# The first loads of an attention + SwiGLU kernel: which row and which weight slice lead which DMA queue, and one transposition placed a K tile sooner

## The chip, the cores and the metric

The kernel runs on one core of a Trainium2 chip. The metric is the device time in microseconds (us) of one execution; less is better. The engines are named as in the profile: PE (TensorE matmuls), PEld (its weight loads), DVE (VectorE), ACT (ScalarE), POOL (GpSimd) and SP (SyncE, which issues DMAs here). ACT can issue DMAs too, on a queue of its own.

## The reference

A layer norm feeds two branches, and both are added to the input. Shapes: S = 2048 tokens, D = 576, F = 4608, 32 heads of 18, a window of 8 keys with a dilation of 2; all tensors are bf16.

```python
xn = layernorm(x)                                   # over D, no scale or bias
q, k, v = split_heads(xn @ wqkv)                    # wqkv: 576 x 1728
# token s looks at tokens s, s-2, ..., s-14 (masked below 0)
o = softmax(q . k[window] * 18**-0.5) @ v[window]   # per head
out = x + o @ wo + (silu(xn @ w_gate) * (xn @ w_up)) @ w_down
```

## The kernel before

**Tiling.** The 2048 tokens are 16 "rows" of 128 tokens (token p * 16 + r is partition p of row r). Four rows make a chunk `c`. Three phases follow one another on PE: the QKV projection of all 16 rows (`qkv_ps`, L301), then, for each of four chunks, gate and up (`g_ps`, L601) and the down projection together with the attention's output projection (`d_ps`, L630). The attention itself runs on DVE beside the FFN matmuls.

**The QKV phase.** The contraction over D = 576 has four K tiles of 128 and a remainder of 64. `wqkv` is loaded by K tile: `load_w(eng, kt)` (L147) brings slice `kt`, 128 x 1728, 432 KB; for `kt` = 4 it brings the remainder in two DMAs of 108 KB to the two halves of the partitions. `load_x(eng, j)` (L144) brings x row `j`, 128 x 576, 144 KB. The argument `eng` is the engine whose queue issues the DMA; each queue keeps its order. In the profile the x rows are the tile `wd` and the weight slices the tile `hT`, because they lie in memory that the FFN uses later. Before the change the order was:

```python
load_x(nc.scalar, 0)
load_x(nc.sync, 1)
load_w(nc.scalar, 1)
load_w(nc.sync, 0)
make_identity(nc, ident[:])
load_w(nc.sync, 2)
load_x(nc.sync, 2)
load_w(nc.sync, 3)
load_w(nc.sync, 4)
load_x(nc.sync, 3)
```

After these come the x rows 4 to 15 in three DMAs of 576 KB on SP (L165), and later the first gate and up weights (`load_gu(0)`, L182 to L185).

**The start on the engines.** The order of work is written out by hand (`manual_schedule`), from L477 on. PE first runs eleven warm-up matmuls on constants (`warm_pe(10, 1)`). Row 0 is a special case: DVE computes its statistics (L214, L218) and subtracts the mean in two parts (L251, first 128 columns, then the rest), POOL fills the padding (L256), PE transposes K tile 0 and then the others (L262), ACT copies the results to `xcT` (L268; `PP` in the profile), and the QKV matmuls of row 0 go through slices 0, 1, 2 (`p_whole`, whole K tiles of 128 rows). Row 0 is scaled by its standard deviation only when its results leave PSUM (`p_evac`, L365 and L367). Row 1 is normalised and transposed between these matmuls; its first K tile is multiplied before slice 3 and the remainder of row 0.

From row 1 on, `p_row` (L321) issues matmuls of half a K tile (64 partitions) in pairs, on the two halves of the array. It goes twice over two pairs of output groups: `swap` 0 and 1, and `i` 0 and 1 within each, with K tiles 0, 4, 1, 2, 3 in the first and 0, 1, 2, 3 in the second pass. K tile 0 is skipped in both passes where `t` is given, which is the case for row 1 alone. The argument `at = (i, kt)` says after which pair of the second pass the function `between` is called; `turn(r)` is such a function and transposes row `r` (`transp_halves`, L274): ten small PE matmuls (L283) into two PSUM banks, then one copy on ACT and one on DVE (L287) to `xnT`. So row 2 is transposed within row 1, row 3 within row 2, row 4 within row 3. Rows from 5 on are transposed by DMA.

PSUM is a ring of eight banks (pool `ps`): a new tile waits until the tile eight places before it has been read.

Of the kernel before, what the change touches and what calls it, by code (L numbers as in the profile page):

```python
# [70 lines left out]
def kernel(  # L71
# [11 lines left out]
    nc = tc.nc  # L83
# [60 lines left out]
    def load_x(eng, j):  # L144
        eng.dma_start(xc_b[0][:, j:j + 1, :], x_v[:, j:j + 1, :])

    def load_w(eng, kt):  # L147
        if kt < 4:
            eng.dma_start(wqkv[:, kt, :], A_wqkv[kt * P:(kt + 1) * P, :])
        else:  # L150
            for i in range(2):
                eng.dma_start(wqkvr[64 * i:64 * i + 64, :], A_wqkv[4 * P:D, 2 * G * i:2 * G * (i + 1)])

    load_x(nc.scalar, 0)
    load_x(nc.sync, 1)
    load_w(nc.scalar, 1)
    load_w(nc.sync, 0)
    make_identity(nc, ident[:])
    load_w(nc.sync, 2)
    load_x(nc.sync, 2)  # L160
# [35 lines left out]
    def new_ps(name):  # L196
        return ps.tile([P, 512], f32, name=name, tag="ps")
# [18 lines left out]
    def ln_aggr(r):  # L216
        c, j = divmod(r, 4)
        nc.vector.bn_aggr(ln[c][2][:, j, :], sums[r][:].rearrange("p c s -> p (c s)"))  # L218
# [55 lines left out]
    def transp_halves(r):  # L274


        c, j = divmod(r, 4)
        xn = ln[c][1]
        pt = [new_ps("pt") for half in range(2)]
        for kt in range(KT):  # L280
            for half in range(2):
                rows = slice(64 * half, 64 * half + 64)
                nc.tensor.matmul(pt[half][:, kt * 64:(kt + 1) * 64], xn[rows, j, kt * P:(kt + 1) * P],  # L283
                                 ident[rows, rows], start=True, stop=True)
        for half, eng in enumerate((nc.scalar.copy, nc.vector.tensor_copy)):
            lo = r * P + 64 * half
            eng(xnT[:, :, lo:lo + 64], pt[half][:, 0:KT * 64].rearrange("p (k t) -> p k t", t=64))  # L287
# [11 lines left out]
    def p_mm(t, g, kt, half, r, start, stop):  # L299
        rows = slice(0, P) if half is None else slice(64 * half, 64 * half + 64)  # L300
        return nc.tensor.matmul(t[g][:, 0:G], xT_of(r)[rows, kt, :], w_at(g, kt, rows),  # L301
                                start=start, stop=stop)
# [10 lines left out]
    def fence_after(mm):  # L313
        f = nc.gpsimd.engine_nop()
        tc.add_manual_dep(f.ins, mm.ins.name, SYNC, reason="first half done")
        return f

    def fence_before(mm, f):
        tc.add_manual_dep(mm.ins, f.ins.name, SYNC, reason="banks change row tiles")

    def p_row(r, between=None, at=(0, 1), t=None):  # L321


        done = t is not None
        t = t or [None] * NG
        fence = {}
        for swap in range(2):
            for i in range(2):
                for kt in (0, 1, 2, 3) if swap else (0, 4, 1, 2, 3):
                    if done and kt == 0:  # L330
                        continue
                    for half in range(2):
                        g = i + 2 * (half ^ swap)
                        if t[g] is None:
                            t[g] = new_ps("qkv_ps")
                        mm = p_mm(t, g, kt, half, r, swap == 0 and kt == 0, swap == 1 and kt == 3)
                        if swap == 0 and kt == 3 and half == 1:
                            fence[i] = fence_after(mm)
                        if swap and kt == (1 if done else 0) and half == 0:
                            fence_before(mm, fence[i])  # L340
                    if swap and (i, kt) == at and between is not None:
                        between()
        return t
# [130 lines left out]
    def turn(r):  # L474
        return lambda: transp_halves(r)
# [32 lines left out]
    u = [None] * NG  # L508
# [11 lines left out]
    load_gu(0)  # L520
    transp_dma(0)

    p_row(1, turn(2), (0, 2), u)
    ln_aggr(3)
    p_evac(1, u, (0, 1, 2), dve=(1, 2))
    ln_sqrt(3)
# [188 lines left out]
```

## Time and profile before

| | us |
|---|---|
| median of 3 runs (503.34 to 504.67) | 503.36 |
| the profiled execution's own time | 503.82 |
| its span, first to last instruction | 502.0 |
| busy time of PE / DVE / ACT / POOL in it | 498.1 / 329.0 / 200.5 / 2.6 |
| first QKV matmul starts, on the span's scale | 6.06 |
| last QKV matmul ends, gate and up begin | 60.19 |

The span is what the profile's time scale covers; 1.8 us of the execution's time lie around it. "SPq" and "ACTq" are the instruction queues of SP and ACT, where DMAs are issued; q1 and q10 are the DMA queues of SP and ACT. A row of the timeline gives start and length in us, engine, line, operation, output and input with shapes, a count, and, in brackets, for how long the engine was idle before it and what ended that. A run of equal instructions is merged to one row.

### The profile page before, as it was taken

What the parts mean: (1) busy time and instruction counts of PE and PEld (TensorE: products, weight loads), DVE (VectorE), ACT (ScalarE), POOL (GpSimd) and SP (SyncE); (2) the same over time, 40 slices, a digit from 0 to 9 for tenths busy, and PEclk for the clock granted to TensorE, in tenths of its full rate; (3) what the DMA queues carried; (4) which work ended last, traced back from release to release, by engine and by line L of the source; (5) the groups of instructions that cost most, each with busy time, mean ns of one, the idle gap of its engine ahead of it and who ended that gap; (6) DMA issues with size and microseconds to landing.
All of it is one profiled execution on the core that took longest, in us unless ns stands there. A gap on an engine that the chain in (4) does not pass through costs nothing.

```text
span 502.0 us, 13267 instructions
## 1 busy us (share of the span) xinstructions
PE 498.1 (99%) x5795; PEld 330.5 (66%) x5795; DVE 329.0 (66%) x478; ACT 200.5 (40%) x415; POOL 2.6 (1%) x9
## 2 busy tenths in 40 slices
PE   9999999999999999999999999999999999999997
PEld 4666655555799755555899655555999555557996
DVE  5888598898999698999898139995980222221001
ACT  4756657644400255554300445557000454553000
POOL 2000000000000000000000000000000000000000
PEclk9999999999999999999999999999999999999999
DMA  8889988789921045536621154465600335453100
GB/s 313 219 206 228 307 280 280 220 273 309 233 82 61 25 136 193 191 106 225 161 69 43 29 185 146 139 189 157 136 25 14 100 114 178 155 177 38 29 14 25
DMA packets 77186, 75.42 MB, mean 150 GB/s; under 512 B 22708, under 2 KB 72528, under 8 KB 77128
## 3 DMA queue, kind: packets, MB, share of 16 engines
q1 hardware_dynamic: 76840, 73.98, 49.7%
q8 instruction: 45, 0.74, 0.6%
q10 hardware_dynamic: 288, 0.59, 0.4%
q14 instruction: 13, 0.11, 0.1%
HBM read 58.76 MB, written 5.90 MB: 129 GB/s over the span
## 4 chain that ended last, share of the span: by engine, by line
PE 99%; DVE 0%; issue 0%
PE g_ps L601 56%; PE d_ps L630 32%; PE qkv_ps L301 11%; PE warm_ps L174 1%; PE pt L262 0%; DVE ot L644 0%; PE pt L283 0%; PE warm_ps L262 0%; PE warm_ps L177 0%
## 5 line engine op out<-in xcount | busy, mean ns | idle before, releaser
L601 PE MATMUL g_ps<-xnT,gu 64*128 64x512 bf16 x2592 | 280.4, 376 | 0.0
L601 PEld LDWEIGHTS <-gu 64*128 64x128 bf16 x2592 | 147.7, 94 | 131.3
L612 ACT ACTIVATE sg<-g_ps 128x512 bf16<-128x512 f32 x144 | 87.3, 606 | 156.6 <-PE g_ps L601 156.6
L630 PE MATMUL d_ps<-wd,hT 64*128 64x288 bf16 x2304 | 146.9, 283 | 0.0
L630 PEld LDWEIGHTS <-hT 64*128 64x128 bf16 x2304 | 131.3, 94 | 10.5
L614 DVE TENSOR_TENSOR hT<-sg,uc 128x512 bf16<-128x512 bf16 x144 | 60.0, 418 | 93.8 <-ACT uc L613 93.6
L613 ACT CAST uc<-g_ps 128x512 bf16<-128x512 f32 x144 | 85.2, 592 | 0.0
L414 DVE TENSOR_REDUCE PP<-PP 128x64 f32<-128x1152 bf16 x64 | 84.9, 1345 | 0.4
L301 PE MATMUL qkv_ps<-hT,xnT 64*128 64x432 bf16 (+1 forms) x536 | 50.2, 343 | 0.0
L409 DVE TENSOR_TENSOR PP<-QO,Kr 128x2304 bf16<-128x2304 bf16 (+1 forms) x35 | 43.5, 1249 | 7.2 <-DMA Kr<-hT 6.9
L642 DVE TENSOR_TENSOR ot<-d_ps,xr 128x288 bf16<-128x288 f32 x30 | 12.3, 451 | 51.1 <-PE d_ps L630 51.1
L441 DVE TENSOR_TENSOR PP<-Vr,A 128x2304 bf16<-128x2304 bf16 (+1 forms) x35 | 43.2, 1250 | 0.4
L301 PEld LDWEIGHTS <-xnT 64*128 64x128 bf16 (+1 forms) x536 | 30.1, 94 | 18.5 <-ACT xnT L287 0.4
L446 DVE TENSOR_TENSOR PP<-PP 128x2304 bf16<-128x2304 bf16 x24 | 32.5, 1353 | 0.3
L612 ACT ACT_TABLE_LOAD x5 | 6.4, 1283 | 47.3 <-PE g_ps L601 47.2
L630 PE MATMUL d_ps<-wo,xnT 64*128 64x288 bf16 x288 | 23.4, 283 | 0.0
L363 ACT CAST hT<-qkv_ps 128x288 bf16<-128x288 f32 (+2 forms) x58 | 21.2, 428 | 0.5 <-DMA kv_d<-hT 0.5
L630 PEld LDWEIGHTS <-xnT 64*128 64x128 bf16 x288 | 16.4, 94 | 1.2
L434 ACT ACTIVATE PP<-PP 128x1024 f32<-128x1024 f32 x4 | 4.2, 1057 | 31.2 <-DVE PP L430 31.2
L644 ACT CAST ot<-d_ps 128x288 bf16<-128x288 f32 x1 | 0.4, 399 | 38.8 <-PE d_ps L630 38.8
L363 ACT CAST QO<-qkv_ps 128x432 bf16<-128x432 f32 (+1 forms) x30 | 12.3, 410 | 7.4 <-PE qkv_ps L301 7.4
L214 DVE BATCH_NORM_STATS2 stats<-wd 128x6 f32<-128x288 bf16 x32 | 12.9, 444 | 2.9 <-DMA wd<-in_A_x_dram 2.6
(53 smaller groups left out, 91.3 us busy)
## 6 DMA issues: line engine op xcount, KB each, us to landing
gu<-in_B_w_gate_dram SPq DMA_DIRECT2D x36, 512.0 KB, 3.8
gu<-in_B_w_up_dram SPq DMA_DIRECT2D x36, 512.0 KB, 5.1
wd<-in_B_w_down_dram SPq DMA_DIRECT2D x9, 576.0 KB, 6.0
kv_d<-hT SPq DMA_DIRECT2D x5, 576.0 KB, 6.4
gu<-in_B_w_gate_dram SPq DMA_DIRECT2D x36, 64.0 KB, 4.7
gu<-in_B_w_up_dram SPq DMA_DIRECT2D x36, 64.0 KB, 4.4
xr<-in_A_x_dram SPq DMA_DIRECT2D x8, 288.0 KB, 5.1
out_dram<-ot SPq DMA_DIRECT2D x16, 144.0 KB, 1.8
```

The source lines that it names most:

```text
L214: nc.vector.bn_stats(sums[r][:, k, :], xc[:, j, k * HALF:(k + 1) * HALF])
L301: return nc.tensor.matmul(t[g][:, 0:G], xT_of(r)[rows, kt, :], w_at(g, kt, rows), start=start, stop=stop)
L363: (nc.vector.tensor_copy if n in dve else nc.scalar.copy)(*parts[n])
L409: nc.vector.tensor_tensor(prod[:, a:b], QO[:, RT * tt + a:RT * tt + b, :], Kr[:, s:s + b - a, :], op=ALU.mult)
L414: nc.vector.tensor_reduce(L[:, w, rs], prod[:, rs].rearrange("p r (h d) -> p r h d", d=DH), axis=AX.X, op=ALU.add)
L441: nc.vector.tensor_tensor(dst[:, a:b], Vr[:, s:s + b - a, :].rearrange("p r (d h) -> p r d h", h=H), A[:, w, a:b].unsqueeze(2).to_broadcas ...
L446: nc.vector.tensor_tensor(dst, acc, pv, op=ALU.add)
L601: mm = nc.tensor.matmul(ring_ps[j][b][:], gu[rows, slot, k, fc], xnT[rows, kt, tok], start=(swap == 0 and kt == 0), stop=(swap == 1 and kt ...
L612: nc.scalar.activation(sg[:], t[0][:], ACT.Silu)
L613: nc.scalar.copy(uc[:], t[1][:])
L614: nc.vector.tensor_tensor(hT[:, ch * FC + j, :], sg[:], uc[:], op=ALU.mult)
L630: mm = nc.tensor.matmul(t[sub][h][:, 0:HALF], a[rows], w[rows, h * HALF:(h + 1) * HALF], start=(swap == 0 and n == 0), stop=(swap == 1 and ...
```

## The change

Four loads at the head of the two queues change place. x row 0 is issued by SP instead of ACT, ahead of row 1. Slice 0 is issued by ACT, as its first and only load, instead of by SP after row 1. Slice 1 goes from ACT to SP, after row 1. All other loads keep their order on SP. And `turn(2)` is called after K tile 1 of the second pass of row 1, not after K tile 2.

```diff
-    load_x(nc.scalar, 0)
+    load_x(nc.sync, 0)
+    load_w(nc.scalar, 0)
     load_x(nc.sync, 1)
-    load_w(nc.scalar, 1)
-    load_w(nc.sync, 0)
+    load_w(nc.sync, 1)
     make_identity(nc, ident[:])
     load_w(nc.sync, 2)
     load_x(nc.sync, 2)
@@
-    p_row(1, turn(2), (0, 2), u)
+    p_row(1, turn(2), (0, 1), u)
     ln_aggr(3)
```

## The prediction

> **What bounds the kernel now.** I read the page first, then the chain of waits in order of time, then the timeline of the first 20 us, because the diff touches nothing later.
>
> The page's first and fourth parts:
>
> ```profile
> span 502.0 us, 13267 instructions
> PE 498.1 (99%) x5795; PEld 330.5 (66%) x5795; DVE 329.0 (66%) x478; ACT 200.5 (40%) x415; POOL 2.6 (1%) x9
> ...
> PE 99%; DVE 0%; issue 0%
> ```
>
> PE is the chain. The chain in order of time shows where it could still lose anything:
>
> ```profile
> 0.76 4.42 PE warm_ps L174 x10
> 5.18 0.11 PE warm_ps L177
> 5.29 0.21 PE pt L262
> ...
> 6.13 2.25 PE qkv_ps L301 x10
> ...
> 19.67 40.52 PE qkv_ps L301 x444
> 60.19 69.93 PE g_ps L601 x648
> ```
>
> From 19.67 on there is no gap: 444 half-row matmuls in 40.52 us is 0.0913 each, 0.1825 a pair. So the time is (start of the first QKV matmul) + (fixed PE work) + (small stalls before 20 us). Only the first and last term can change, and nothing in this diff shortens the fixed work. The timeline of the start, all engines:
>
> ```profile
> 3.81 0.82 DVE L214 BATCH_NORM_STATS2 stats<-wd 128x6 f32<-128x288 bf16 x2 [2.63 <-DMA wd<-in_A_x_dram]
> ...
> 5.21 0.10 PEld L262 LDWEIGHTS <-wd 128*128 128x128 bf16 x1 [0.51 <-DVE wd L251]
> ...
> 5.54 0.27 ACT L268 COPY PP<-pt 128x128 bf16<-128x128 bf16 x1 [0.34 <-PE pt L262]
> ...
> 5.85 0.31 PEld L301 LDWEIGHTS <-PP 128*128 128x128 bf16 x2
> 6.06 2.31 PE L301 MATMUL qkv_ps<-hT,PP 128*128 128x432 bf16 x10
> ...
> 6.37 0.15 PEld L301 LDWEIGHTS <-PP 128*128 128x128 bf16 x1 [0.21 <-issue]
> ...
> 6.73 1.21 PEld L301 LDWEIGHTS <-PP 128*128 128x128 bf16 x7 [0.21 <-issue]
> ```
>
> A serial line runs from the landing of x row 0 to the first QKV matmul: statistics at 3.81, centring, transposition 5.21, copy 5.54 to 5.81, weight load 5.85, matmul 6.06. DVE sat idle 2.63 us for that landing. Two smaller losses are visible. The load at 5.85 was ready, yet its matmul began at 6.06: in the trace's semaphore records the last share of slice 0 (`wqkv[:, 0]`) landed at 6.02. And the first three matmuls start 0.31, 0.36 and 0.20 apart, where 0.182 is the later pace: the array was still slow until about 6.73 (the warm-up matmuls of 512 columns, 0.43 apart, are at that slow pace throughout). The weight-load timeline shows the place of the second edit:
>
> ```profile
> 12.83 0.49 PEld L301 LDWEIGHTS <-xnT 64*128 64x128 bf16 x8
> 13.70 1.97 PEld L301 LDWEIGHTS <-xnT 64*128 64x128 bf16 x24 [0.37 <-ACT xnT L287]
> ...
> 16.03 3.06 PEld L301 LDWEIGHTS <-xnT 64*128 64x128 bf16 x36
> ```
>
> Row 2's first load waits for the two copies of its own transposition; rows 3 and 4, turned after (0,1), go straight on (36 loads from 16.03 with no idle).
>
> **x row 0 goes to SP, slice 0 leads on ACT's queue.** Before, two 144 KB rows led the two queues:
>
> ```profile
> wd<-in_A_x_dram ACTq DMA_DIRECT2D x1, 144.0 KB, 3.1
> wd<-in_A_x_dram SPq DMA_DIRECT2D x1, 144.0 KB, 3.2
> ```
>
> (issue 0.72 each, landings 3.78 and 3.96). The packet records show one packet per row of a tile, eight to an engine, a 1152-byte one every 0.047 us and a 3456-byte one every 0.132, and the two queues taking turns packet by packet: on one engine q10, q1, q10, q1 at 2.526, 2.573, 2.620, 2.667, and with long packets q1, q10, q1 at 3.256, 3.388, 3.520. So x row 0 shared with x row 1 for 16 x 0.047 = 0.75 us; now it shares with slice 0: 8 x (0.047 + 0.132) = 1.43. That is 0.68 later. SP's row landed 0.18 behind ACT's of the same issue time; I add half, 0.09. Sum +0.77. High end 0.68 + 0.18 = 0.86. Low end: SP served entirely ahead of ACT, so that row 0 skips the 8 x 0.047 of the other row: -0.38. I take 0.77, since the taking of turns is in the records. Landing then about 4.55.
>
> [...]
>
> Slice 0, issued at 0.72 and not 1.18 and no longer behind a row, finishes with row 0, near 4.6. Its wait (5.85 to 6.06) goes: -0.20, ends 0 and -0.21. The DVE, ACT and PE line between simply shifts with row 0. First QKV matmul: 6.06 + 0.77 - 0.20 = 6.63.
>
> **What else moves in the queues.** SP now issues x0, x1, w1, w2 ...: from w2 on everything is one issue later (0.40 to 0.46 a row). The transfers run back to back from 2.6 us, so the backlog covers this: w3 was issued at 2.63 and landed at 9.09. The bytes ahead of each slice are the old ones in another order. Slice 1 becomes the fourth item in, as slice 0 was: about 6.1, used by the fifth matmul (7.12 before, about 7.5 now). Row 1 lands 8 x 0.047 after row 0, about 4.95; DVE wants it at 5.39 + 0.77. Slack of the rest, landing against first use: slice 2 7.16/7.85, row 2 7.59/8.72, slice 3 9.09/9.69, the remainder 9.83/10.52, row 3 10.19/11.98, the next x block 11.62/14.90. Slice 3 is thinnest, 0.60, and its user itself comes later; were that cover gone, each microsecond would be one on PE. SP's later issues wait for landings of the first ones (that at 3.80 for row 0's semaphore), so the last pieces are issued about 1 us later, still 3 us ahead of their packets' turn; `gu`, behind them, is wanted at 60. ACT loses one issue, and its table load (1.64, 1.28 us) moves 0.4 ahead; its first use is at 4.90. All this I cost at nothing.
>
> **Clock.** The slow pace ended at about 6.73 in the profiled execution. With the first matmul at 6.63, the three slow starts (0.87 us for 0.55 of work) shrink to one tenth: -0.27, if the pace rises at the same moment. Ends 0 (an execution in which it had risen before 6.06 loses nothing now) and -0.33.
>
> **Row 2 a K tile sooner.** The ten transpositions go in one pair earlier: 0.18. Row 1's last matmul before the boundary starts 0.32 before row 2's first, not 0.18, so 0.13 is lost. Between transposition and boundary lay four pairs of matmuls (`p_row` skips K tile 0 of a row that is begun): 4 x 0.18 + 0.13 = 0.86 was needed, and five pairs give 0.91. All 0.13 comes back, just. Covers: row 2's input was ready at 10.98, transposed from 12.54; ACT's and DVE's earlier work ends at 12.60 and 12.79, and the copies can start near 12.85. The two PSUM banks are row 0's first two, last read by the first of ACT's pair at 11.69 (until 12.19): against 12.36 that cover is thin, 0.17, and if it goes the transpositions wait and the 0.13 stays lost. Ends 0 and -0.14.
>
> **Sum.** Against the profiled execution (503.82, span 502.0): +0.77 - 0.20 - 0.27 - 0.13 = +0.17, 504.0. The median of the runs, 503.36, lies 0.46 lower, which fits executions whose array was fast before 6.06; for those the clock term is nil and the sum is +0.44. With half of the clock term: 503.36 + 0.44 - 0.14 = 503.66, say **503.7**. 0.3% is 1.5 us, about what a measurement of this kernel can tell from no change: this is no change.
>
> **Rivals.**
>
> *The clock stays slow (slower).* Warm-up ends at 5.08 by its own pace, and the first transposition began at 5.21. Now PE would sit idle from 5.08 to about 5.95. If whatever raises the pace wants PE kept busy, those 0.87 us, where 0.13 stood, can cost it. Price from rows: before, it took from 0.76 to 6.73, 6.0 us of nearly steady work. If the earning starts afresh after the gap, the pace rises at up to 11.9 and half of 6.63 to 11.9 is lost, 2.6; if half is kept, about 1.3 to 1.6. So 505.0 to 506.3, about 505.3. It decides from the point where the idle stretch spoils the count; the trace shows only that 0.13 + 0.20 + 0.14 of gaps did not. One of the three runs is 1.3 above the others, which may be this very thing happening now and then.
>
> [...]
>
> *Row 0 isn't held up.* If SP's small packets win, the term of 0.77 falls to between 0 and -0.38, and the gain is 0.2 + 0.13 and up to 0.38: 502.7 to 503.2, still within 0.3%. Against it: the alternating packets.
>
> *A real gain over 1.5 us* has no source: all losses before 20 us add up to less than 1.
>
> **Numbers.** Forecast as summed 0.51; row 0 not held up 0.11; clock stays slow 0.35; something unforeseen ahead 0.03. The first two are "same", 0.62; slower 0.35; faster 0.03. The forecast's own range is 503.1 to 504.4 (ends of the terms). To leave out no more than 2 in 10 the range takes in most of the clock case: 503.0 to 505.7.
>
> **What would show it.** Right: DVE's first statistics near 4.6; first QKV matmul near 6.6, with no gap between its load and itself; weight loads from then on 0.18 apart; no idle ahead of row 2's loads; `g_ps` starting about 0.2 later than 60.19. Wrong: statistics at 3.8 (no sharing); QKV matmuls 0.36 apart until 9 or 12 (clock); an idle PEld before the matmuls of slice 1 or 3 (late slices).

## The result and the profile after

The changed kernel took 505.94 us (median of 6 runs, 505.21 to 506.62), the kernel before in the same comparison 503.62 (503.32 to 504.67). The ratio is 1.0045, 95% interval 1.0033 to 1.0057: slower by 2.3 us, and outside the range of 503.0 to 505.7. A second comparison, below, gave 504.72 (12 runs, 504.14 to 506.91) against 503.81, ratio 1.0027 (1.0014 to 1.0040). So it is slower both times; how much, we shall see, is drawn anew in each execution.

The profiled execution took 506.01, span 504.2. Its chain in order of time, to be read against that of before:

```profile
0.72 4.27 DMA wd<-in_A_x_dram
...
5.01 0.83 DVE stats L214 x2
...
6.73 0.40 PE pt L262 x4
7.13 3.21 PE qkv_ps L301 x10
...
11.33 3.65 PE qkv_ps L301 x30
...
21.80 40.52 PE qkv_ps L301 x444
62.32 69.93 PE g_ps L601 x648
```

Before, the last row stood at 60.19: the whole difference, 2.13, is there when gate and up begin. Three pieces account for it. The first ten QKV matmuls begin at 7.13 instead of 6.13: +1.00. From there to the row at 11.33 (9.02 before) it is 4.20 instead of 2.89: +1.31. From there to 21.80 (19.67 before) it is 10.47 instead of 10.65: -0.18. The first is x row 0, 1.20 later, less slice 0's wait of 0.20, which is gone; the chain now starts with a DMA. The second is the clock, and the third the earlier turn of row 2.

The timeline of weight loads shows the second piece:

```profile
6.42 0.10 PEld L262 LDWEIGHTS <-wd 128*128 128x128 bf16 x1 [1.98 <-DVE wd L251]
6.73 0.23 PEld L262 LDWEIGHTS <-wd 128*128 128x128 bf16 x4 [0.21 <-DVE wd L251]
7.01 0.75 PEld L301 LDWEIGHTS <-PP 128*128 128x128 bf16 x5
7.97 0.15 PEld L301 LDWEIGHTS <-PP 128*128 128x128 bf16 x1 [0.21 <-issue]
8.33 0.15 PEld L301 LDWEIGHTS <-PP 128*128 128x128 bf16 x1 [0.21 <-issue]
8.69 0.15 PEld L301 LDWEIGHTS <-PP 128*128 128x128 bf16 x1 [0.21 <-issue]
```

Five loads go at the fast pace, then each is 0.36 after the last, with nothing to wait for ("issue"). The view by stretches says why (stretch, its length, PE's busy time and matmuls, the granted clock as a share of full speed, the busy share of the DMA engines, GB/s):

```profile
6.00:7.00 1.00, 0.50 (x5) 1.00 0.99 380
7.00:8.00 1.00, 1.00 (x8) 0.76 1.06 400
8.00:9.00 1.00, 1.00 (x4) 0.50 1.03 313
9.00:10.00 1.00, 1.00 (x4) 0.50 1.12 266
10.00:11.00 1.00, 1.00 (x6) 0.53 1.04 399
11.00:12.00 1.00, 1.00 (x9) 1.00 1.01 406
```

The clock, fast from 4.10, was halved from 7.52 to 10.93 by the trace's clock record. Between 4.78, when the warm-up ended, and 6.42 PE had been idle (the chain's owner was DMA). So in this execution the fast clock wasn't late, as the clock rival had it: it came and was taken away again. Each run's mean granted clock shows how often. A halved stretch of 3.41 us in 504 makes it 0.997, and two of the six runs (506.01, 506.62) have that. The other four have 1.0, which doesn't exclude a late first release: in the profile before, the clock record begins with the release at 6.76, and the mean is 1.000 although the first three QKV matmuls start 0.31 and 0.36 apart.

### The profile page after: what moved, and what is told of

Read it like the earlier page. It is cut to its first block, busy times and chain, and to the rows that moved or that the text cites. A ratio compares the mean times of both kernels' runs of the same rounds, so it can differ in the third digit from the quotient of the medians.

```text
span 504.2 us, 13267 instructions
## 1 busy us (share of the span) xinstructions
PE 498.6 (99%) x5795; PEld 285.3 (57%) x5795; DVE 329.1 (65%) x478; ACT 200.6 (40%) x415; POOL 2.6 (1%) x9
## 4 chain that ended last, share of the span: by engine, by line
PE 98%; DMA 1%; DVE 0%; issue 0%
PE g_ps L601 55%; PE d_ps L630 32%; PE qkv_ps L301 11%; DMA wd<-in_A_x_dram 1%; DVE stats L214 0%; PE pt L262 0%; DVE wd L251 0%; DVE ot L644 0%; PE pt L283 0%; DVE mv L218 0%; PE warm_ps L262 0%
## 5 line engine op out<-in xcount | busy, mean ns | idle before, releaser
L601 PEld LDWEIGHTS <-gu 64*128 64x128 bf16 x2592 | 127.0, 94 | 152.1
L630 PEld LDWEIGHTS <-hT 64*128 64x128 bf16 x2304 | 113.1, 94 | 28.7
L301 PEld LDWEIGHTS <-xnT 64*128 64x128 bf16 (+1 forms) x536 | 26.1, 94 | 22.3 <-ACT xnT L287 0.2
L630 PEld LDWEIGHTS <-xnT 64*128 64x128 bf16 x288 | 14.1, 94 | 3.6 <-DMA xnT<-QO 0.2
```

What stands on the lines that cost most here:

```text
L601: mm = nc.tensor.matmul(ring_ps[j][b][:], gu[rows, slot, k, fc], xnT[rows, kt, tok], start=(swap == 0 and kt == 0), stop=(swap == 1 and kt ...
L630: mm = nc.tensor.matmul(t[sub][h][:, 0:HALF], a[rows], w[rows, h * HALF:(h + 1) * HALF], start=(swap == 0 and n == 0), stop=(swap == 1 and ...
```

## The experiments

Each was timed beside the kernel before, in 7 to 12 runs. E10, E11, E8 and E9 share one comparison, E1 to E4 another, E5 to E7 a third; E12 has its own. Theory A: row 0 lands about 1 us later because it takes turns with long packets, and the idle PE then costs the fast clock in many executions. The rivals B to F are in the expectations.

**E1, the loads alone.**

```diff
-    p_row(1, turn(2), (0, 1), u)
+    p_row(1, turn(2), (0, 2), u)      # on the changed kernel
```

> The change with its load order alone; row 2 is turned after (0, 2) as before. Theory A (two terms: row 0 lands about 1 us later because it takes turns with slice 0's long packets, and the idle PE then loses the fast clock for a stretch): the whole loss of 2.3 us is in the loads, so this stands 2.3 to 2.6 us above the kernel before, with a stall of about 0.13 ahead of row 2's loads again. Rival B (the earlier turn of row 2 does harm, by banks or by a late copy): this comes back towards the kernel before, under +1.5 us.

504.74 (504.09 to 505.79), ratio 1.0016 (1.0007 to 1.0025). Only +1.0: under theory A's window, and as rival B had it, 1.2 under the changed kernel. In the profiled run (505.79) the clock was first released at 9.71, against 6.76 in the kernel before: here the clock was late, in the form that the rival had. Side by side, though, the two kernels are alike:

**E10 and E11, the changed kernel and its loads alone, once more and together.**

> The changed kernel itself once more, beside its loads alone and beside a variant without the gap. Theory A (row 0 later by about 1 us; the idle PE then costs the fast clock in many but not all executions): between 504.1 (clock kept) and 506.6, median 504.7 to 506.0, and the same as its loads alone within 0.4. Rival B (the early turn of row 2 does harm together with the late loads): over 1 us slower than its loads alone, as the first two comparisons, made apart, had it (505.9 against 504.7).

> The loads alone, row 2 turned after (0, 2), beside the changed kernel. Theory A: 0 to 0.3 us above the changed kernel on the same chip (the stall of 0.13 is back), 504.7 to 506.0. Rival B: over 1 us below it.

504.72 and 504.82 (504.28 to 506.02; ratio 1.0020, 1.0010 to 1.0029). Rival B is out. The runs of the changed kernel fall into two groups: seven lie between 504.14 and 504.75, five between 505.63 and 506.91, and none between. (With the loads alone the groups are less sharp: E1 and E11 have single runs at 505.00, 505.07 and 505.24.) Two of the upper five have a mean clock of 0.997; the others, with 1.0, were not profiled. The profiled run, of 504.14, kept its clock:

```profile
6.24 0.10 PEld L262 LDWEIGHTS <-wd 128*128 128x128 bf16 x1 [1.69 <-DVE wd L251]
6.55 0.23 PEld L262 LDWEIGHTS <-wd 128*128 128x128 bf16 x4 [0.21 <-DVE wd L251]
6.83 1.57 PEld L301 LDWEIGHTS <-PP 128*128 128x128 bf16 x10
```

All ten loads go at the fast pace. Its `g_ps` starts at 60.50 against 62.32, so one kernel differs from itself by 1.82 us: 0.18 is row 0 (statistics at 4.84, not 5.01), and 1.67 lies between the start of the QKV matmuls and the second mark (2.53 here, 4.20 there). Its idle stretch on PE is a little shorter. The matmuls, first in the changed kernel's first profile, then here:

```profile
6.42 0.70 PE L262 MATMUL pt<-ident,wd 128*128 128x128 bf16 x5 [1.65 <-DVE wd L251]
6.25 0.71 PE L262 MATMUL pt<-ident,wd 128*128 128x128 bf16 x5 [1.36 <-DVE wd L251]
```

And PE's busy time (third figure) in the 3.41 us after each release of the clock:

```profile
4.10:7.52 3.42, 1.70 (x12) 1.00 1.03 375
4.33:7.74 3.41, 1.97 (x13) 1.00 1.01 385
```

With 1.70 busy the clock was lost at the end of the stretch, with 1.97 it was kept. All six runs of the first comparison lie above 505.2. By E10's share, five in twelve, six out of six would come up about once in 200 times, so the share probably differs between comparisons; what sets it was not tested. Setting that high median against E1's, taken apart from it, misled.

**E2, the turn alone.**

```diff
-    p_row(1, turn(2), (0, 2), u)      # on the kernel before
+    p_row(1, turn(2), (0, 1), u)
```

> The kernel before with only the turn of row 2 one K tile sooner. Theory A: the idle of 0.37 ahead of row 2's weight loads shrinks or goes, -0.13 us, which is less than the spread of the runs (1.3 us), so: no change within 0.3%. Rival B: slower by 0.3 us or more, with a new wait at row 2's transposition.

503.51 (503.31 to 505.39) against 503.76, ratio 1.0001 (0.9991 to 1.0010): nothing measurable. Its profiled run, 504.65, shows that a high run need not be the clock's: released at 3.78, it reached gate and up 0.33 before the kernel before did (59.86), and then lost 1.1 us in the first down projection, where PE waited for a transposition by DMA:

```profile
135.13 0.79 PE L630 MATMUL d_ps<-wo,xnT 64*128 64x288 bf16 x10 [0.93 <-DMA xnT<-QO]
```

The size of the turn is in the traces of E10 and E11, which both kept the clock: from the 9.5 us mark to the 444 matmuls 10.50 (9.48 to 19.98) with the early turn, 10.66 (9.50 to 20.16) without.

**E3, the gap alone.** Loads, landings and first QKV matmul of the kernel before, with three warm-up matmuls fewer.

```diff
-    warm_pe(10, 1)                    # on the kernel before
+    warm_pe(7, 1)
```

> The kernel before with its own loads and 7 instead of 10 warm-up matmuls of 512 columns. PE is then idle from about 3.85 to 5.2, 1.35 us, which is the length of the gap in the changed kernel (5.1 to 6.4), while row 0, the slices and the first QKV matmul (6.06) stay in place. Theory A: the gap alone costs the fast clock for a stretch of the first 12 us in most executions, QKV matmuls 0.36 apart there, and the time rises by 1.0 to 1.9 us. Rival C (the clock's price comes from the heavier DMA traffic or the later slices, not from idle PE): the same time as before, within 0.5 us.

504.44 (503.42 to 506.15), ratio 1.0011 (0.9999 to 1.0023). Two groups again: six runs between 503.42 and 503.88, six between 505.01 and 506.15; of the 35 runs of before beside it, none is over 504.71 (beside E5 to E7 and E12 one run each is over 505: 505.07 of 25, 505.70 of 16). The profiled run (505.01) is of the upper group:

```profile
3.27 0.15 PEld L177 LDWEIGHTS <-const-bfloat16-1.0 128*128 128x128 bf16 x1 [0.28 <-issue]
5.15 0.10 PEld L262 LDWEIGHTS <-wd 128*128 128x128 bf16 x1 [1.73 <-DVE wd L251]
...
6.64 0.15 PEld L301 LDWEIGHTS <-PP 128*128 128x128 bf16 x1 [0.21 <-issue]
...
8.80 0.15 PEld L301 LDWEIGHTS <-PP 128*128 128x128 bf16 x1 [0.21 <-issue]
```

Row 0's statistics start at 3.74, nothing is late, and the matmuls still go 0.36 apart until 9.16: the clock was first released at 9.26, late, as the rival had it. Idle PE alone does it; six of twelve executions are in the upper group. Theory A's "most" was too much, and the interval of the ratio, over all runs, just reaches 1; the groups are what shows it. Rival C falls.

**E4 and E8, the gap filled.** E4 warms up longer, blindly; E8 adds matmuls that begin when row 0 lands.

```diff
-    warm_pe(10, 1)                    # on the changed kernel
+    warm_pe(14, 1)                    # E4
```

```diff
     warm_pe(10, 1)                    # on the changed kernel, E8
+    for i in range(4):
+        nc.tensor.matmul(wp[:], xc_b[0][:, 0, 0:P], xc_b[0][:, 0, 0:512], start=True, stop=True)
```

> The changed kernel with 14 instead of 10 warm-up matmuls, which fill the gap until row 0 is ready: at the slow pace they end at about 6.84, 0.4 after the first transposition could begin, at the fast pace (from 4.1) at about 5.4. Theory A: the late landing stays (first QKV matmul at 7.0 to 7.4), but the clock holds, so about 1 us comes back: 504.3 to 505.2, against 505.9 of the changed kernel. Rival C: no gain, 505.9 or up to 0.4 more.

> The changed kernel plus four filler matmuls of 512 columns on PE after the warm-up, which read x row 0 and so begin when it lands (about 5.0) and run until 5.9 (fast) or 6.7 (slow). PE is then idle for half a microsecond at most before row 0's transposition. Theory A: the clock term goes, only the late row 0 is left: 504.0 to 504.8, median near 504.4, spread under 1 us. Rival C (idle PE isn't what costs the clock): as the changed kernel, 505 to 506.5, or more by the fillers.

E4: 504.86 (503.91 to 506.19), ratio 1.0020 (1.0010 to 1.0030). The median is in the window, but it is no better than E10's, and the spread, 2.3, is little smaller than E10's 2.8. In its profile the warm-up runs at the slow pace, ends at 6.78 and holds the transposition up; that a fast warm-up would end early and leave a gap follows from its pace, but no trace shows it. It settles nothing. E8: 504.44, and all eleven runs between 504.18 and 504.91 (ratio 1.0009, 1.0001 to 1.0018), where the changed kernel on the same chip reached 506.91. The upper group is gone. Means give the price of the clock: 505.18 for E10's twelve runs less 504.48 for E8's eleven, 0.7 us an execution; E10's two groups agree: 1.8 apart in the mean, times five runs in twelve, is 0.76. What is left over E9's 503.56 (below), 0.9, is the late row and what it brings along. In E8's profile that includes slice 3, flagged as thinnest: 15 of its 16 shares were in by 9.40, the last landed at 10.54, and PE waited for it.

```profile
10.12 0.10 PEld L301 LDWEIGHTS <-PP 128*128 128x128 bf16 x1
10.59 0.46 PEld L301 LDWEIGHTS <-PP 128*128 128x128 bf16 x3 [0.36 <-issue]
```

**E5 and E9, row 1 moved ahead of slice 0.** E9 also has one warm-up matmul more, `warm_pe(11, 1)`.

```diff
     load_x(nc.sync, 0)                # on the changed kernel
-    load_w(nc.scalar, 0)
-    load_x(nc.sync, 1)
+    load_x(nc.scalar, 1)
+    load_w(nc.scalar, 0)
     load_w(nc.sync, 1)
```

> The changed kernel with row 1 moved ahead of slice 0 on ACT's queue: x row 0 leads SP, x row 1 leads ACT, then slice 0 on ACT and slice 1 on SP (the order of before with the queues exchanged), and row 2's early turn. Theory A (turns by packet): row 0 shares with row 1's short packets again and lands at 3.8 to 4.0, the gap on PE is 0.1 to 0.3, the first QKV matmul starts at 5.9 to 6.1: 503.2 to 503.8. Rival D (SP's queue itself is the slow one for row 0, whatever shares with it): row 0 lands later than 4.5 and the time stays over 505.

> Both rows lead the two queues, slice 0 on ACT, slice 1 on SP, row 2 turned early, and 11 instead of 10 warm-up matmuls, which shorten the idle stretch ahead of row 0's transposition. Theory A: the clock is held in more executions than with 10, so median 503.3 to 503.6 (503.56 with 10), the upper end of the runs under 504.7. If the longer warm-up delays the transposition in slow-clock executions, +0.1 to +0.2 instead.

E5: 503.56 (503.41 to 505.45), ratio 0.9996 (0.9988 to 1.0005). Row 0 lands at 3.93, only 0.15 later than at the head of ACT's queue (3.78 in before), so SP's queue isn't the cause (rival D); its mate is. E9: 503.56, all runs between 503.37 and 503.90, while before, beside it, ran from 503.31 to 504.95 (503.81); ratio 0.9991 (0.9983 to 1.0000). The interval reaches 1, so no gain is shown. Its lowest run is no lower than that of before; what it lacks is upper runs.

**E6, slice 0 in short packets.**

```diff
-    load_w(nc.scalar, 0)              # on the changed kernel
+    for i in range(3):
+        nc.scalar.dma_start(wqkv[:, 0, i * D:(i + 1) * D], A_wqkv[0:P, i * D:(i + 1) * D])
```

> The changed kernel with slice 0 on ACT's queue cut into three DMAs of 576 columns, so that its packets are 1152 bytes like those of row 0; bytes, order and queues are those of the change. Theory A (the queues take turns packet by packet, so long packets hold up short ones): row 0 lands 0.5 to 0.8 us sooner than the 4.99 of the changed kernel, at 4.1 to 4.5, slice 0 at 5.0 to 5.4 and without delay to PE; 503.6 to 505.0 according to whether the clock holds. Rival E (row 0 waits because slice 0's DMA is ahead of it in some shared issue or start-up stage, not for the packets' length): row 0 still lands at about 4.9, over 505.3.

The mechanism is confirmed, the time is not. Row 0 lands at 3.60, not 4.99, beside the same bytes in the same order: the row length of the queue's mate sets it, and rival E is out. But 505.50 (504.44 to 509.21), ratio 1.0045 (1.0025 to 1.0065). Now slice 0's last third is late. It shares with the 3456-byte packets of slice 1 on SP; 15 of its 16 shares are in by 5.97, the last lands at 7.48, which turns alone don't explain. PE waits for it after two matmuls:

```profile
5.62 0.30 PEld L302 LDWEIGHTS <-PP 128*128 128x128 bf16 x3
7.52 1.19 PEld L302 LDWEIGHTS <-PP 128*128 128x128 bf16 x7 [1.60 <-issue]
```

This run (504.84) kept its clock; the three that make the upper end, 508.86 to 509.21, have a mean clock of 0.992 or 0.993. By the same working as above, an estimate from these means, it was halved there for 7 to 8 us.

**E7, row 0 in two halves, and E12, slice 0's thirds on both queues**, two tries for a better order.

```diff
-    load_x(nc.sync, 0)                # E7, on the changed kernel; warm_pe(9, 1)
+    nc.sync.dma_start(xc_b[0][0:64, 0:1, :], x_v[0:64, 0:1, :])
+    nc.scalar.dma_start(xc_b[0][64:P, 0:1, :], x_v[64:P, 0:1, :])
```

```diff
-    load_w(nc.scalar, 0)              # E12, on the changed kernel: w0 in thirds
+    load_w0(nc.scalar, 0)
+    load_w0(nc.scalar, 1)
+    load_w0(nc.sync, 2)
```

> Row 0 is cut in two halves of 64 partitions, one at the head of each queue; then slice 0 on ACT, row 1 and slice 1 on SP; row 2's early turn; 9 warm-up matmuls instead of 10, to end before the earlier transposition. Theory A: row 0 has only its own 8 short packets per engine, in two streams, and lands at 3.4 to 3.6; slice 0 at about 5.4; first QKV matmul at 5.5 to 5.8; no long gap. 502.7 to 503.4, 0.2 to 0.9 us under the kernel before. Rival F (the start-up of the queues, about 3 us from issue to landing, sets the landing, not the packets): lands at 3.8 as before, and the time is that of before less the 0.13 of row 2 and up to 0.2 of slice 0's wait.

> Slice 0 in three DMAs of 576 columns, two on ACT's queue and the third on SP's behind row 0, so that no piece has to take turns with slice 1's long packets (in the variant with all three on ACT the third landed only at 7.48 and PE waited 1.60 us for it). Row 0 leads SP, row 1 and slice 1 follow the third piece, row 2 early, 10 warm-up matmuls. Theory A: row 0 lands at 3.6 to 3.8, slice 0 by 5.0 to 5.4, first QKV matmul at 5.6 to 5.8, 0.3 sooner than with both rows in the lead: 503.1 to 503.5. Against it: if the pieces share with slice 1 after all, slice 0 lands past 6 and the time is 503.6 or more.

Both missed. E7: 505.59 (504.82 to 505.98), ratio 1.0027 (1.0016 to 1.0039). ACT's half lands at 3.08, but SP's still at 3.72 (about as rival F had it), and everything behind it suffers: the issue of a half row takes SP 0.59, the next 0.81, slice 1 lands at 8.15 (5.98 in E5), slice 3 at 11.62 (8.87); in the first 14 us the DMA engines moved 271 GB/s against 322 in E5. E12: 505.33 (504.53 to 506.51), ratio 1.0031 (1.0020 to 1.0042). The head is as expected: row 0 lands at 3.68, slice 0's last third at 4.41, and the first QKV matmul starts at 5.82. But row 1 lands at 5.76, slices 1, 2 and 3 at 6.92, 8.07 and 10.25, and the weight loads wait 0.42, 0.51 and 0.42 for these slices. Another 1.0 is lost in the first down projection, as in E2's profiled run. Why the transfers behind run slower in these two wasn't tried out. The packet records show where: between 2.7 and 9 us, ten packets in E7 and nine in E12 took 0.47 to 1.0 us each, where a 3456-byte one mostly takes 0.135. The changed kernel, E1, E4, E6, E8, E10 and E11 have one to six of over 0.45; before, E2, E3, E5 and E9 have none.

## Why the prediction was wrong

**The choice of case failed, at the step "Clock".** The forecast summed -0.27 for slow starts that the late beginning would skip. That took the moment of the release as fixed, although the sum's own +0.77 made PE idle longer ahead of it. The loss was left as a rival at 0.35. The runs showed that idle PE alone can cost the clock (E3, six of twelve runs over 505.0) and that filling the gap keeps it (E8, no run over 504.91). With the gap it is a draw at every execution (five of twelve in E10, by their times), with a mean price of 0.7 us there (E10 less E8). The rival had the cause right, idle PE ahead of row 0's transposition; of the gap it had too little, 0.87 against 1.65 in the profile. Its price, 1.3 to 2.6, holds the 1.31 of the second piece and the 1.67 between two profiles of the kernel. Its form is one of two: E1's and E3's profiles show a late release (9.71 and 9.26), while in the changed kernel's profile the clock was lost again. There 1.65 us of idle was enough, and in E10's profile 1.36 us did no harm. That the second median, 504.72, lies inside the range is no merit of the sum, which had no such loss in it.

**Row 0: right mechanism, too small.** +0.77 was forecast, with a high end of 0.86; the statistics start at 5.01 instead of 3.81, +1.20, and at 4.77 to 4.97 in the five other profiles with these loads (E1, E4, E8, E10, E11), +0.96 to +1.16. The term that was mis-sized is the sharing with slice 0's long packets, 0.68 in the sum. E5 has row 0 on SP too, with a short-row mate, and lands it at 3.93, not 4.99: the sharing costs 1.06. SP's queue costs 0.15 (3.93 against 3.78), put at 0.09. In E4's profile SP's first packet even left before ACT's, at 1.75 against 1.97, and row 0 still landed at 4.74, where E9's, first out too, landed at 3.53. Why the sharing costs more than eight long packets is not shown; four of ACT's first packets in the changed kernel's trace took 0.55 to 0.93 us each, which may be part of it. The turns that the sum took are in the changed kernel's packet records: of 99 rows of 1152 bytes on SP's queue between 2.4 and 3.9 us that took the usual 0.05 us, 70 are followed 0.047 us after their start by a row on ACT's queue, and 18 by one of their own. (The records don't name the DMA engine; about ten matches of either kind would come by chance.)

**Right:** slice 0's wait of 0.20 is gone (load and matmul both at 7.01); the turn of row 2 gave 0.16, forecast 0.13; slices 1 and 2 stayed hidden. Slice 3's cover of 0.60 held in the changed kernel's profiles but not in E8's. Without the clock's loss the change costs 504.14 less 503.31, the lowest runs of E10 and of before: 0.8, where the same sum gave 0.44.

**The spread was the hint that I undervalued.** I named the one run 1.3 above the others and still took the median as the place to start from. Which cause raised that run is open: none of the kernel before's high runs was profiled, and E2's high run lost its time in the down projection, not by the clock. A few runs of a kernel with two outcomes 1.5 us apart put the median in either.

## What to carry to other kernels

A transfer that starts the critical chain is best paired with transfers whose rows are as short as its own: the two queues took turns row by row here, and a mate with rows of 3456 bytes, not 1152, cost 1.06 us (4.99 against 3.93). A wait moved to the head of a kernel can be paid twice if PE idles in it, as in the profile of the changed kernel (+1.00 for the row, +1.31 for the clock): keep PE fed until the real work begins. Filler that starts when the data lands (E8) removed the upper runs; a longer fixed warm-up did not in E4, while E9, with row 0 early and eleven matmuls, had none either. And look at the single runs and their mean clock: a gap in their distribution shows that there are two outcomes, which the profile of one run can't, and a profile from each group then shows the cause.

## What the runs showed of the hardware

In the changed kernel's profile the clock fell 1.1 us after the end of an idle stretch of 1.65 us and came back after 3.41. The 3.41 us ahead of each first release were at least four fifths busy (2.74 us from 0.09 to 3.50 in E7, 3.02 from 0.37 to 3.78 in E2). Stretches of that length with 2.25 to 2.59 us busy, each one length ahead of a first release, didn't bring it (2.43 to 5.85 in E3, 2.88 to 6.30 in E1, up to 3.35 in before). The clock was kept after less: 1.83 us busy in E7 (6.91 to 10.33), 1.84 in E6 and 1.97 in E10 (3.41 us from their releases at 3.87 and 4.33); after 1.70 in the changed kernel it was lost. That the busy time in such a stretch decides is the author's estimate from these few executions; no run shows a limit. The two DMA queues took turns row by row: rows of 1152 bytes in the profile before 0.047 us apart, rows of 3456 bytes 0.132 apart, and a row of ACT's queue 0.047 after 70 of the 99 short ones in the changed kernel's. Row 0 landed at 3.53 to 3.93 where its mate's rows are as short as its own (before, E2, E3, E5, E6, E9, E12) and at 4.74 to 4.99 where they are 3456 bytes long (the changed kernel twice, E1, E4, E8, E11).
